# Attention inside a fused attention and expert kernel: the first score, transposition and value product of a group wait for the whole group

## The chip, the cores and the metric

The kernel runs on one core of one Trainium2 chip. Its time is what the device takes for one execution of the whole program, in microseconds (us); lower is better. TensorE (PE in the profile, PEld for its weight loads) multiplies matrices, VectorE (DVE), ScalarE (ACT) and GpSimd (POOL) work elementwise, SyncE (SP) issues transfers. Each engine works through its own queue in order, and engines wait for each other by semaphores.

## The reference

Three stages follow each other; what is changed lies in the first.

```python
scores = scale * np.matmul(q, k.transpose(0, 1, 3, 2))     # 4 sequences, 8 heads, 576 rows, 64 wide
scores = np.where(mask, scores + bias[None], -1000000000.0) # causal, window 128, slope per head
scores = scores - np.max(scores, axis=-1, keepdims=True)
attn = np.exp(scores)
attn = attn / (np.sum(attn, axis=-1, keepdims=True) + 1e-09)
out = np.matmul(attn, v)                                    # then reshaped to 2304 x 512
...
out += P[:, e:e + 1] * (np.maximum(x @ w1[e], 0.0) @ w2[e]) # 8 experts, gates P balanced by 8 rounds
...
return np.maximum(0.01 * h, h) @ w_out                      # h = x @ w_in
```

## The kernel before

The 2304 rows are 18 tiles of 128. Attention takes a tile in two groups of four heads (`steps`, 36 groups in all, `quad` 0 and 1). In a group, head `h = 4 * quad + 2 * n + r`: `n` is 0 or 1, and `r` says in which half of the 128 partitions the 64 values of the head lie (0: partitions 0 to 63, 1: 64 to 127), which is also the half of TensorE's rows that its score product uses.

For each group the kernel does the following.

- `scores` (L223 to L250): four products in float32 (L238), ordered n outer and r inner, write two PSUM tiles `s[0]` and `s[1]`, one for each `r`, each with both `n`. There are two such buffers, so the tiles of one group must be free before the next group writes them. Then for each head VectorE adds the distances and takes the row's minimum (L243, negated scores, so the minimum stands for the maximum), writing `e[r]`, and ScalarE takes the exponential of it in place with a sum (L247). Five buffers hold `e` tiles; a group takes two, and they come free when the group's transpositions have read them. A product shows as two TensorE records, since float32 goes through in two passes: a group has 8 records on L238.
- `probs_T` (L265): for each `r`, four transpositions on TensorE (L273) into `pt`, and one ScalarE copy to `pb` (L275).
- `values` (L278): eight products (L288), n outer, then key block, then r inner, into one PSUM tile `o` for the 8 heads of a tile; 16 records a group. A tile that starts a sequence has one key block, so its scores are 128 wide instead of 256 and its group has half the transpositions and value products.
- After the second group of a tile, `inverses` (L252) spreads the inverted row sums (L260), and VectorE scales the result into `acc` (L296).

The main loop (from L894 on) writes group s+1's scores ahead of group s's transpositions and values. Between them, `filling` sets in other jobs: the scaling and splitting of the first expert's weights (L553, L427, L428), then from the fifth tile on, steps of the first expert's two products (`a_steps`, L702, and `b_steps`, L819) for the tiles that are ready. All these jobs are emitted before attention ends; afterwards the kernel goes on with the other experts and the last network, where L702 and L819 make up nearly all of TensorE's work.

The order of the instructions in each engine's queue is not that of the program text alone. The kernel is built with `schedule_with_timeline_sim=True`: a planner goes through a simulated time line, and what stands earlier in the text goes first among what it holds ready. An instruction that it holds not yet ready is passed by others on its engine. The order is fixed when the kernel is built, and the chip keeps to it.

Of the kernel before, what the change touches and what calls it, by code (L numbers as in the profile page):

```python
# [13 lines left out]
AF = mybir.ActivationFunctionType  # L14
# [17 lines left out]
def attn_moe_kernel(  # L32
# [12 lines left out]
    nc = tc.nc  # L45
    P = 128
# [31 lines left out]
    ident = const.tile([P, P], F32, name="ident")  # L78
# [27 lines left out]
    for h in range(H):  # L106
        r = 64 * (h % 2)
# [6 lines left out]
    pools = {}  # L114

    anchors = {}

    def anchor():
        ins = nc.cur_bb.bb.instructions[-1]
        anchors[ins.engine] = ins  # L120
# [71 lines left out]
    st = {}  # L192
# [30 lines left out]
    def scores(i, quad):  # L223
        c = st[i]
        kb, qs = c["kb"], c["qs"]
        W = P * len(kb)
        c0 = 2 * P - W
        mn = ap2.tile([P, 4], F32, tag="mn", name="mn")
        if quad == 0:
            c["sm"] = ap2.tile([P, H], F32, tag="sm", name="sm")  # L230
        sm = c["sm"]
        s = [ps_s.tile([P, 2, 2 * P], F32, tag="s", name="s") for _ in range(2)]
        e = [ap1.tile([P, 2, 2 * P], F32, tag="e", bufs=5, name="e") for _ in range(2)]
        c[quad] = dict(e=e)
        for n in range(2):
            for r in range(2):
                h = 4 * quad + 2 * n + r
                nc.tensor.matmul(s[r][:, n, 0:W], qs[64 * r:64 * r + 64, h // 2, :],  # L238
                                 c["k"][64 * r:64 * r + 64, h // 2, 0:W], start=True, stop=True)
        for n in range(2):  # L240
            for r in range(2):
                h = 4 * quad + 2 * n + r
                nc.vector.tensor_tensor_reduce(  # L243
                    out=e[r][:, n, 0:W], in0=s[r][:, n, 0:W], in1=c["bias"][:, c0:], scale=2.0 ** (-8.0 * (h + 1) / H),
                    scalar=float(2**41), op0=ALU.add, op1=ALU.min, accum_out=mn[:, 2 * n + r:2 * n + r + 1],
                )
                nc.scalar.activation(  # L247
                    out=e[r][:, n, 0:W], in_=e[r][:, n, 0:W], func=AF.Exp, bias=mn[:, 2 * n + r:2 * n + r + 1],
                    scale=-1.0, accum_out=sm[:, h:h + 1],
                )  # L250

    def inverses(i):  # L252

        c = st[i]
        sm = c["sm"]
        nc.scalar.activation(out=sm, in_=sm, func=AF.Copy, bias=EPS)
        nc.vector.reciprocal(out=sm, in_=sm)
        rt = ps_t.tile([P, NP, P], F32, tag="pt", name="rt")
        for h in range(H):
            nc.tensor.matmul(rt[64 * (h % 2):64 * (h % 2) + 64, h // 2, :], sm[:, h:h + 1].to_broadcast([P, D]), ident,  # L260
                             start=True, stop=True)
        rb = c["rb"] = ap1.tile([P, NP, P], F32, tag="rb", name="rb")
        nc.scalar.activation(out=rb, in_=rt, func=AF.Copy)

    def probs_T(i, quad):  # L265
        c = st[i][quad]
        nb = len(st[i]["kb"])
        c["pb"] = []
        for r in range(2):
            pt = ps_t.tile([P, 2, 2, P], F32, tag="pt", name="pt")  # L270
            for n in range(2):
                for b in range(nb):
                    nc.tensor.transpose(pt[:, n, b, :], c["e"][r][:, n, b * P:(b + 1) * P], ident)  # L273
            pb = ap3.tile([P, 2, 2, P], F32, tag="pb", name="pb")
            nc.scalar.activation(out=pb[:, :, 0:nb, :], in_=pt[:, :, 0:nb, :], func=AF.Copy)  # L275
            c["pb"].append(pb)

    def values(i, quad):  # L278
        kb = st[i]["kb"]
        if quad == 0:  # L280
            st[i]["o"] = ps_o.tile([P, NP, P], F32, tag="o", name="o")
        o = st[i]["o"]
        pb = st[i][quad]["pb"]
        for n in range(2):
            for b, j in enumerate(kb):
                for r in range(2):
                    h = 4 * quad + 2 * n + r
                    nc.tensor.matmul(  # L288
                        o[64 * r:64 * r + 64, h // 2, :],
                        st[j]["v"][:, h * D:(h + 1) * D],  # L290
                        pb[r][:, n, b, :],
                        start=(b == 0), stop=(b == len(kb) - 1),
                    )
        if quad == 1:
            p = max(p for p, (t0, n) in enumerate(PAIRS) if t0 <= i)
            nc.vector.scalar_tensor_tensor(out=accT[i], in0=o, scalar=xin[p].sr[:, 0:1], in1=st[i]["rb"],  # L296
                                           op0=ALU.mult, op1=ALU.mult)
# [235 lines left out]
    W = [{}, {}]  # L533
# [342 lines left out]

    nc.sync.dma_start(wg, w_gate.rearrange("(k p) e -> p k e", p=P))
    scores(*steps[0])
    for job in input_scale(0):
        job()  # L880
# [13 lines left out]
    for s, (i, quad) in enumerate(steps):  # L894
# [11 lines left out]
        if s + 1 < len(steps):  # L906
            if quad == 1 and i + 2 < NTILE:
                load_qk(i + 2)
            if quad == 0 and 2 <= i + 1 < NTILE:
                load_v(i + 1)  # L910
            scores(*steps[s + 1])
# [6 lines left out]
        if scales:  # L918
            scales.pop(0)()
        probs_T(i, quad)  # L920
        if quad == 1:
            inverses(i)
        filling(left - 1)
        if scales:
            scales.pop(0)()
        values(i, quad)
    assert not fill
    for _ in range(8):
# [66 lines left out]
    for n, u in enumerate(units + [None]):  # L995
        a, b = [], b_steps(*prev)
# [9 lines left out]
        if prev[1] == ends[prev[0]] and prev[0] + 1 < NC:  # L1006
            k0 = len(b) - 7
            b = [[f] + ([lambda j=k - k0: W[1][prev[0] + 1].at(j)] if k >= k0 else []) for k, f in enumerate(b)]
        else:
            b = [[f] for f in b]  # L1010
# [70 lines left out]
```

## Time and profile before

| What | Value |
|---|---|
| time, median of 3 runs | 1960.12 us (1958.14 to 1960.9) |
| time of the profiled execution | 1959.59 us |
| its span, first to last instruction | 1957.8 us |
| VectorE busy | 1320.9 us (67%) |
| ScalarE busy | 1366.5 us (70%) |
| GpSimd busy | 1327.3 us (68%) |
| attention (L238, first to last start) | 5.0 to 221.8 us |

A busy share is the part of the span in which an engine had an instruction in hand. Matmuls are pipelined: the next one starts before the last one's modelled end, so what a stretch of them costs TensorE is read from one start to the next start, and the busy time of a piece reaches a little over it. A row of the time line merges neighbours of the same kind: `x8` are eight records, `[0.21 <-ACT pb L275]` is idle time before them and what ended it. In the view by windows each engine has its busy time and, in brackets, its instructions.

### The profile page before, as it was taken

How to read it: one execution, taken by the hardware profiler on the slowest of the kernel's cores; microseconds unless marked ns; L12 is line 12 of the kernel's file. 1: busy time of each engine (PE TensorE's matmuls, PEld its weight loads, DVE VectorE, ACT ScalarE, POOL GpSimd, SP SyncE). 2: the span in 40 equal slices, each digit the busy share in tenths (PEclk: the TensorE clock that was granted, in tenths of full speed). 3: DMA queues.
4: the chain of work that ended last, by engine and by line, in shares of the span. 5: the costliest groups of instructions: out<-in, count | busy, mean ns of one | idle time of the engine just before them, and what ended most of it. 6: DMA issues, size and time to landing. Idle time of an engine off the chain costs nothing.

```text
span 1957.8 us, 45103 instructions
## 1 busy us (share of the span) xinstructions
PE 1890.2 (97%) x17725; PEld 1626.5 (83%) x17725; DVE 1320.9 (67%) x3604; ACT 1366.5 (70%) x3123; POOL 1327.3 (68%) x1142
## 2 busy tenths in 40 slices
PE   8999988999999999999999999999999998999998
PEld 6777667888898888889888888889889877889897
DVE  6444466676776767677676767666666777677876
ACT  7977666776767666676767676676666778776764
POOL 3843275868787786878677686775767686666743
PEclk9999999999999999999999999999999999999999
DMA  8432001120211211120111112101000000001001
GB/s 269 125 87 71 12 12 55 39 62 32 82 47 47 66 39 55 39 82 28 66 65 40 55 39 66 44 2 45 23 23 23 23 23 23 24 22 44 2 28 71
DMA packets 57861, 97.80 MB, mean 50 GB/s; under 512 B 3632, under 2 KB 22064, under 8 KB 57648
## 3 DMA queue, kind: packets, MB, share of 16 engines
q1 hardware_dynamic: 57648, 94.92, 14.9%
q8 instruction: 138, 2.26, 0.5%
q14 instruction: 75, 0.61, 0.1%
HBM read 81.81 MB, written 13.11 MB: 48 GB/s over the span
## 4 chain that ended last, share of the span: by engine, by line
PE 78%; ACT 7%; DVE 5%; DMA 5%; POOL 3%; issue 2%; POOLq 0%; SPq 0%; ACTq 0%; DVEq 0%
PE t L819 35%; PE s L702 21%; PE sq L702 15%; DMA raw<-in_moe_w_dram 3%; PE s L238 2%; PE o L288 2%; PE pt L273 1%; ACT junk L550 1%; POOL h L775 1%; DVE s L731 1%; PE rt L260 1%; ACT raw L553 1%; ACT w L427 1%; ACT e L247 1%; ACT xp L427 1%
## 5 line engine op out<-in xcount | busy, mean ns | idle before, releaser
L819 PE MATMUL t<-w,h 128*128 128x256 f16 x7560 | 985.1, 273 | 22.9 <-ACT part L829 10.3
L702 PEld LDWEIGHTS <-w 128*128 128x128 f16 x8400 | 759.1, 98 | 120.3 <-issue 35.0
L819 PEld LDWEIGHTS <-h 128*128 128x128 f16 x7560 | 730.2, 98 | 125.6 <-issue 33.9
L702 PE MATMUL s<-xp,w 128*128 128x256 f16 (+1 forms) x4908 | 620.3, 263 | 20.3 <-ACT q L726 10.4
L832 DVE SCALAR_TENSOR_TENSOR acc<-t,pu,acc 128x256 f32<-128x256 f32 x864 | 407.9, 479 | 220.3 <-PE t L819 173.3
L775 POOL TENSOR_TENSOR h<-s,h 128x1024 f16<-128x1024 f32 x180 | 388.2, 2157 | 136.8 <-ACT h L772 95.7
L702 PE MATMUL sq<-xp,w 128*128 128x256 f16 (+1 forms) x3492 | 447.5, 262 | 6.2 <-ACT q L714 4.5
L830 POOL TENSOR_TENSOR acc<-acc,part 128x256 f32<-128x256 f32 x324 | 235.6, 729 | 292.9 <-ACT part L829 260.6
L428 POOL TENSOR_TENSOR w<-raw,w 128x512 f16<-128x512 f32 x240 | 277.7, 1168 | 42.3 <-ACT w L427 41.9
L731 DVE SCALAR_TENSOR_TENSOR h<-sq,h 128x512 f16<-128x512 f32 (+1 forms) x348 | 190.6, 552 | 82.4 <-ACT h L756 47.6
L829 ACT ACTIVATE part<-t,pu 128x256 f32<-128x256 f32 x324 | 152.5, 471 | 109.0 <-PE t L819 100.1
L772 ACT ACTIVATE h<-s 128x1024 f16<-128x1024 f32 x180 | 189.6, 1053 | 42.2 <-DVE s L731 41.3
L718 DVE SCALAR_TENSOR_TENSOR sq<-sq,q 128x256 f32<-128x256 f32 x348 | 148.4, 427 | 72.0 <-PE sq L702 57.0
L714 ACT ACTIVATE q<-s 128x256 f32<-128x256 f32 x366 | 138.3, 379 | 73.0 <-PE s L702 60.4
L427 ACT ACTIVATE w<-raw 128x512 f16<-128x512 f32 x240 | 148.2, 628 | 8.3 <-PE t L819 6.0
L731 DVE SCALAR_TENSOR_TENSOR s<-sq,s 128x256 f32<-128x256 f32 x348 | 145.1, 417 | 2.1
L750 ACT ACTIVATE h<-sq 128x512 f16<-128x512 f32 x174 | 103.2, 593 | 55.4 <-PE t L819 28.9
L731 DVE SCALAR_TENSOR_TENSOR s<-sq,q 128x256 f32<-128x256 f32 x348 | 130.3, 416 | 12.4 <-ACT q L726 10.6
L550 ACT ACTIVATE junk<-raw 128x512 bf16<-128x512 f32 x160 | 100.2, 626 | 48.2 <-DMA raw<-in_moe_w_dram 47.1
L718 DVE SCALAR_TENSOR_TENSOR sq<-s,q 128x256 f32<-128x256 f32 x174 | 74.5, 428 | 86.6 <-ACT q L714 78.2
L756 ACT ACTIVATE h<-sq 128x256 f16<-128x256 f32 x174 | 65.9, 379 | 65.1 <-DVE sq L718 58.2
L553 ACT ACTIVATE raw<-raw,sr 128x512 f32<-128x512 f32 x160 | 102.4, 714 | 3.8 <-DVE sr L422 3.4
(137 smaller groups left out, 1785.8 us busy)
## 6 DMA issues: line engine op xcount, KB each, us to landing
raw<-in_moe_w_dram SPq DMA_DIRECT2D x32, 1024.0 KB, 5.1
k_t<-in_k_dram SPq DMA_DIRECT2D x16, 512.0 KB, 3.8
raw<-in_moe_w_in_dram SPq DMA_DIRECT2D x16, 512.0 KB, 3.6
raw<-in_moe_w_out_dram SPq DMA_DIRECT2D x16, 512.0 KB, 3.5
q_t<-in_q_dram SPq DMA_DIRECT2D x18, 256.0 KB, 3.7
v_t<-in_v_dram SPq DMA_DIRECT2D x18, 256.0 KB, 2.7
acc<-in_v_dram SPq DMA_DIRECT2D x18, 256.0 KB, 6.6
out_dram<-acc SPq DMA_DIRECT2D x18, 256.0 KB, 2.0
```

The costliest lines, as they stand in the source:

```text
L427: nc.scalar.activation(out=hi, in_=src, func=AF.Copy)
L428: nc.gpsimd.tensor_tensor(out=lo, in0=src, in1=hi, op=ALU.subtract)
L702: nc.tensor.matmul(d[b][:, f, :], t[:, wp, kk, ft * P:(ft + 1) * P], XP[p][:, o, kk, xp, :], start=(i == 0 and f == 0 and j in FIRST), sto ...
L714: nc.scalar.activation(out=q[:, k], in_=ps, func=AF.Copy, scale=CS)
L718: nc.vector.scalar_tensor_tensor(out=block(k), in0=ps, scalar=CS, in1=q[:, k], op0=ALU.mult, op1=ALU.add)
L731: nc.vector.scalar_tensor_tensor(out=out, in0=in0, scalar=sc, in1=in1, op0=op0, op1=op)
L772: nc.scalar.activation(out=h[:, 3:7, 0, :], in_=d["s"], func=AF.Copy)
L775: nc.gpsimd.tensor_tensor(out=h[:, 3:7, 1, :], in0=d["s"], in1=h[:, 3:7, 0, :], op=ALU.subtract)
L819: nc.tensor.matmul(ps, h[:, o, hp, f, tt * P:(tt + 1) * P], w[:, wp, ft, :], start=(i == 0 and j in FIRST), stop=(i == 5), skip_group_chec ...
L829: nc.scalar.activation(out=part, in_=ps, func=AF.Copy, scale=s)
L830: nc.gpsimd.tensor_tensor(out=dst, in0=dst, in1=part, op=ALU.add)
L832: nc.vector.scalar_tensor_tensor(out=dst, in0=ps, scalar=s, in1=dst, op0=ALU.mult, op1=ALU.add)
```

## The change

`behind(ins, other)` makes an instruction wait for another. Four things are done with it or beside it.

- In `scores`, the first product (n = r = 0) waits for the last minimum of the group before.
- The minima and exponentials go r outer and n inner, instead of n outer and r inner: first both heads of `e[0]`, then both of `e[1]`.
- In `probs_T`, the first transposition of each `r` waits for the exponential of the second head of that `r`.
- In `values`, the first product waits for the copy of the second `pb` of its group.

No instruction is added to the arithmetic and none is taken away.

```diff
@@ -115,6 +115,11 @@
 
     anchors = {}
 
+    def behind(ins, other):
+
+        tc.add_manual_dep(ins.ins, other.ins.name, mybir.DependencyInfo(mybir.DependencyClass.Sync, mybir.DependencyReason.DATA),
+                          reason="whole group")
+
     def anchor():
         ins = nc.cur_bb.bb.instructions[-1]
         anchors[ins.engine] = ins
@@ -235,19 +240,23 @@
         for n in range(2):
             for r in range(2):
                 h = 4 * quad + 2 * n + r
-                nc.tensor.matmul(s[r][:, n, 0:W], qs[64 * r:64 * r + 64, h // 2, :],
-                                 c["k"][64 * r:64 * r + 64, h // 2, 0:W], start=True, stop=True)
-        for n in range(2):
-            for r in range(2):
+                ins = nc.tensor.matmul(s[r][:, n, 0:W], qs[64 * r:64 * r + 64, h // 2, :],
+                                       c["k"][64 * r:64 * r + 64, h // 2, 0:W], start=True, stop=True)
+                if n == r == 0 and "minimum" in st:
+                    behind(ins, st["minimum"])
+        exps = c[quad]["exps"] = []
+        for r in range(2):
+            for n in range(2):
                 h = 4 * quad + 2 * n + r
-                nc.vector.tensor_tensor_reduce(
+                st["minimum"] = nc.vector.tensor_tensor_reduce(
                     out=e[r][:, n, 0:W], in0=s[r][:, n, 0:W], in1=c["bias"][:, c0:], scale=2.0 ** (-8.0 * (h + 1) / H),
                     scalar=float(2**41), op0=ALU.add, op1=ALU.min, accum_out=mn[:, 2 * n + r:2 * n + r + 1],
                 )
-                nc.scalar.activation(
+                ins = nc.scalar.activation(
                     out=e[r][:, n, 0:W], in_=e[r][:, n, 0:W], func=AF.Exp, bias=mn[:, 2 * n + r:2 * n + r + 1],
                     scale=-1.0, accum_out=sm[:, h:h + 1],
                 )
+            exps.append(ins)
 
     def inverses(i):
 
@@ -270,9 +279,11 @@
             pt = ps_t.tile([P, 2, 2, P], F32, tag="pt", name="pt")
             for n in range(2):
                 for b in range(nb):
-                    nc.tensor.transpose(pt[:, n, b, :], c["e"][r][:, n, b * P:(b + 1) * P], ident)
+                    ins = nc.tensor.transpose(pt[:, n, b, :], c["e"][r][:, n, b * P:(b + 1) * P], ident)
+                    if n == b == 0:
+                        behind(ins, c["exps"][r])
             pb = ap3.tile([P, 2, 2, P], F32, tag="pb", name="pb")
-            nc.scalar.activation(out=pb[:, :, 0:nb, :], in_=pt[:, :, 0:nb, :], func=AF.Copy)
+            c["copied"] = nc.scalar.activation(out=pb[:, :, 0:nb, :], in_=pt[:, :, 0:nb, :], func=AF.Copy)
             c["pb"].append(pb)
 
     def values(i, quad):
@@ -285,12 +296,14 @@
             for b, j in enumerate(kb):
                 for r in range(2):
                     h = 4 * quad + 2 * n + r
-                    nc.tensor.matmul(
+                    ins = nc.tensor.matmul(
                         o[64 * r:64 * r + 64, h // 2, :],
                         st[j]["v"][:, h * D:(h + 1) * D],
                         pb[r][:, n, b, :],
                         start=(b == 0), stop=(b == len(kb) - 1),
                     )
+                    if n == b == r == 0:
+                        behind(ins, st[i][quad]["copied"])
         if quad == 1:
             p = max(p for p, (t0, n) in enumerate(PAIRS) if t0 <= i)
             nc.vector.scalar_tensor_tensor(out=accT[i], in0=o, scalar=xin[p].sr[:, 0:1], in1=st[i]["rb"],
```

## Rows read from the trace of the kernel before

**Rows 1.** The page's busy times over the span: share, instructions.

```profile
PE 1890.2 (97%) x17725; PEld 1626.5 (83%) x17725; DVE 1320.9 (67%) x3604; ACT 1366.5 (70%) x3123; POOL 1327.3 (68%) x1142
```

**Rows 2.** Windows: length, busy PE, PEld, DVE, ACT, POOL (instructions); clock, DMA, GB/s.

```profile
0.00:80.00 80.00, 72.05 (x528) 51.09 (x529) 42.17 (x202) 67.74 (x207) 45.48 (x61) 1.00 0.66 211
80.00:235.00 155.00, 153.40 (x1443) 112.97 (x1442) 79.29 (x279) 110.45 (x321) 55.06 (x49) 1.00 0.24 69
235.00:300.00 65.00, 52.22 (x529) 42.56 (x528) 36.62 (x109) 42.29 (x98) 45.48 (x40) 0.95 0.03 9
```

**Rows 3.** Windows of the score products alone (L238): PE, PEld.

```profile
0.00:80.00 80.00, 31.53 (x124) 19.61 (x124) 1.00 0.66 211
80.00:235.00 155.00, 34.83 (x164) 20.10 (x164) 1.00 0.24 69
```

**Rows 4.** Windows of the value products alone (L288): PE, PEld.

```profile
0.00:80.00 80.00, 17.62 (x176) 12.32 (x176) 1.00 0.66 211
80.00:235.00 155.00, 33.97 (x368) 23.45 (x368) 1.00 0.24 69
```

**Rows 5.** Time line of TensorE, 105 to 135 us: start, length, what, records.

```profile
108.91 0.43 PE L288 MATMUL o<-pb,v_t 128*64 128x128 f32 x2
109.28 0.66 PE L273 MATMUL pt<-ident,e 128*128 128x128 f32 x4
...
111.42 1.09 PE L288 MATMUL o<-pb,v_t 128*64 128x128 f32 x14
112.44 0.66 PE L273 MATMUL pt<-ident,e 128*128 128x128 f32 x4
...
113.25 1.14 PE L238 MATMUL s<-k_t,qs 64*128 64x256 f32 x8
114.32 0.88 PE L260 MATMUL rt<-ident,sm 128*64 128x128 f32 x12
...
115.81 1.13 PE L238 MATMUL s<-k_t,qs 64*128 64x256 f32 x4
...
123.17 1.13 PE L238 MATMUL s<-k_t,qs 64*128 64x256 f32 x4
124.23 0.83 PE L819 MATMUL t<-w,h 128*128 128x256 f16 x6
```

**Rows 6.** Time line of all engines, 155 to 170 us: TensorE's rows.

```profile
160.50 1.09 PE L288 MATMUL o<-pb,v_t 128*64 128x128 f32 x16
...
161.53 0.87 PE L273 MATMUL pt<-ident,e 128*128 128x128 f32 x6
...
163.53 1.13 PE L238 MATMUL s<-k_t,qs 64*128 64x256 f32 x6
...
164.59 0.50 PE L819 MATMUL t<-w,h 128*128 128x256 f16 x3
...
165.03 0.70 PE L238 MATMUL s<-k_t,qs 64*128 64x256 f32 x2
...
165.65 0.87 PE L260 MATMUL rt<-ident,sm 128*64 128x128 f32 x10
```

**Rows 7.** Windows of the minima alone (L243, with their reads): DVE.

```profile
80.00:235.00 155.00, 31.62 (x172) 1.00 0.24 69
```

**Rows 8.** Windows of the exponentials alone (L247, with reads): ACT.

```profile
80.00:235.00 155.00, 46.17 (x172) 1.00 0.24 69
```

**Rows 9.** TensorE's separate waits for L238: least/median/most ns.

```profile
L238 PEldq EVENT_SEMAPHORE  x16: 51/51/2665, 4.6 to 206.7; - x16
```

**Rows 10.** Waits from 0 to 80 us: total us, times, longest.

```profile
DVE e L243 <- PE pt L273: 9.5, 4, 5.6
```

**Rows 11.** Chain of waits, 225 to 300 us: start, us, what.

```profile
232.55 0.67 DVE acc L296
233.37 2.59 ACT xp L427 x6
...
241.98 2.88 DVE sx L474 x3
```

## The prediction, made before the changed kernel was built or run

> **What bounds the kernel now.** I read the page's busy times first: TensorE has an instruction in hand 97% of the span and no other engine over 70% [rows 1]. The change touches only attention, so I cut its stage out by windows [rows 2]. The reader is to see three parts. Up to 80 us TensorE has only 528 records and ScalarE is busy 67.7 of 80 us. From 80 to 235 us TensorE is busy 153.4 of 155 us with 1443 records, ScalarE 110.5, VectorE 79.3, GpSimd 55.1: here TensorE's queue is the bound, because attention's products share it with the first expert's (L702, L819). From 235 to 300 us TensorE falls to 52.2 of 65.
>
> Then I looked at what TensorE's time is spent on, in the time line, from one start to the next. A whole score group, eight records that alternate between the two halves of the rows, takes 114.32 - 113.25 = 1.07 us. Half a group, four records that all use one half of the rows, takes 124.23 - 123.17 = 1.06 us [rows 5]. So a half costs as much as a whole: products on different row halves run beside each other, products on the same half one after the other. The halves of that group started at 115.81 and 123.17, 7.36 us apart, with other work between. The planner had held `s[0]` ready first, sent its two products alone, and `s[1]`'s later.
>
> The value products have the same fault in small. A whole group of 16 takes 161.53 - 160.50 = 1.03 us [rows 6]. Sent as 2 (waiting for the second `pb`) and later 14, it takes 109.28 - 108.91 = 0.37 and 112.44 - 111.42 = 1.02, so 1.39 us [rows 5], 0.36 more.
>
> **The change part by part.** *First score waits for the last minimum of the group before.* That minimum frees `s[1]`, so at that moment both PSUM tiles are free and all four products are ready at once; in the program's order they alternate the row halves. Price now: L238 is busy 34.83 us from 80 to 235 us in 164 records [rows 3], which is 20.5 groups. Whole they would be busy 20.5 x 1.14 = 23.4 us (1.14 is the busy time of the x8 row of [rows 5]). The difference is 11.5 us, in about 11 pieces too many, and each piece's busy time reaches 0.07 us over the next start (1.13 against 1.06), so 11.5 - 0.8 = 10.7 us of TensorE's queue. A second kind of cut may stay. Five of the twenty groups there are cut into six and two records with an expert's work between them, as at 163.53 and 165.03: both halves were ready and the planner still set something in. That costs 164.59 - 163.53 + 165.65 - 165.03 = 1.68 us against 1.07 [rows 6], 0.61 each, 3.0 in all, which I leave in. Left: 7.7 us.
>
> *First value product waits for the second copy.* L288 is busy 33.97 us in 368 records from 80 to 235 us [rows 4], 23 groups; whole they would be busy 23 x 1.09 = 25.1 us [rows 6]. Of the 8.9 us difference, about 21 pieces too many count 0.07 us each twice (1.09 against 1.02 in [rows 5]), 1.5 us. Left: 7.4 us. The copy of the second `pb` ends the wait of the other 14 now, so they start no later; the first two are late by 0.37 us at most.
>
> *First transposition waits for the second exponential.* Four transpositions stay the unit, as most of them stand now (x4 in [rows 5]), so I count nothing. Bounds: 2 us gained where pairs now go alone, 2 us lost where a pair could have filled a hole.
>
> *Minima by row halves.* Four minima and four exponentials a group, before and after: nothing added. A head's minimum takes 31.62 / 86 = 0.37 us and its exponential 46.17 / 86 = 0.54 us [rows 7, 8]. The exponentials that the first transpositions need come second instead of third, 0.54 us sooner; those of the other half come at the same time. Nothing on the path of a full TensorE: 0, with 0.37 us a group as the bound either way.
>
> *The waits themselves.* 35 on scores, 72 on transpositions and 36 on value products. Each first instruction waits for the same engine already, so I expect a higher count in a wait that is there. If each became a separate wait of TensorE's sequencer it would cost 143 x 0.051 = 7.3 us [rows 9]; I take 0, since only 16 such stand before L238's 288 records now, and keep 7.3 as the end. Behind a waiting score stand, in TensorE's own queue, whatever the planner put there: transpositions, values, L702, L819; for these wait ScalarE's copies and VectorE's evacuations. From 80 us on the planner has expert products to put ahead of the score; that is the cover. Without it a group loses the lead of its first half: two minima and two exponentials, 2 x 0.37 + 2 x 0.54 = 1.8 us.
>
> *Before 80 us.* L238 is busy 31.53 us in 124 records where 15.5 whole groups would be 17.7, so up to 13.8 us lie there too [rows 3], and about 3 more in the values. But ScalarE is busy 67.7 of 80 us [rows 2], and attention waits for its exponentials and copies. The Trainium skill, TensorEngine Tiling (Array Packing), section Performance Considerations, says that tiling speeds up TensorE but not the emptying of PSUM, which may become the bound. By that rule these 80 us give nothing, by TensorE's rows up to 17; ScalarE's row here is on the rule's side. I take 0 and keep 10 for the range, since ScalarE's first 80 us hold weight splitting that could be done after.
>
> *After attention.* The chain from 232.55 us goes from the last scaling into `acc` to the splits of the last tiles (ACT xp, DVE sx) [rows 11]. It begins when attention ends and moves with it, so what attention gains is not given back there.
>
> **The sum.** 7.7 + 7.4 = 15.1 us off the profiled execution's 1959.59 (span 1957.8 plus 1.8 around it): 1944.5 us. The median of the runs shown is 0.5 us over the profiled one, so I forecast **1945 us**. What is late next: with 15 us less, ScalarE is busy 110.5 of 140 us, 79%, still under TensorE.
>
> **The rivals.**
> *The order stays cut.* The planner still sets expert steps and older attention work between the products, because these stand earlier in the text. For it: the five groups in six and two. Against it: only half-ready tiles make the four-and-four cut, and this goes. If half of the gain stays away: 1959.6 - 7.5 = 1952 us.
> *ScalarE or the seam takes the gain.* ScalarE's queue, already full before 80 us, holds `pb` and `e` back, or the weights of the next expert end the stretch from 235 to 300 us whatever attention does. For it: TensorE is only 80% busy there [rows 2]. Against it: the chain there starts at attention's last tile [rows 11], and ScalarE has 45 us free between 80 and 235. Then 1960 us, within 2 of before.
> *The lost lead counts before 80 us.* Here hardly any expert product can cover a waiting score. A group's last minima can themselves wait for TensorE, since `e` buffers come free only with transpositions: 9.5 us in four waits, the longest 5.6 [rows 10]. Now a whole score group stands behind such a minimum, where half of it went ahead before. If each of the 16 groups there loses the 1.8 us worked out above, that is 29 us against 15 gained: 1974 us at the worst, 1967 if three quarters are lost. It decides from 15.1 / 16 = 0.94 us a group on. Against it: the second half waited for that minimum before too, and a group's values need both halves.
> *It does nothing.* If the planner already held the scores for whole tiles, nothing would move; the four-and-four cuts speak against that, and I give this no chance of its own beside the second rival.
>
> **How the numbers follow.** Forecast (most pieces become whole) 0.58, order stays cut 0.18, gain taken away 0.12, lost lead 0.12. About 0.2%, 3.9 us, is what a measurement of this kernel can tell from no change. The first two are faster by more than that, with a little left over in the second: faster 0.75. The third is the same, with that little: same 0.14. The fourth, less its mildest cases: slower 0.11. The range goes down to what the stretch before 80 us could add and the cuts in six and two could still give, 1944.5 - 10 - 3 = 1931.5, so 1931; up, over the second rival and the third, to 1963, which holds the mildest third of the lost lead. About 0.08 lies above it and 0.07 below.
>
> **What would show it.** The score group as x8 in TensorE's time line with 1.07 us to the next start, and L238 busy some 24 to 27 us instead of 34.83 for 164 records; L288 as x16, busy near 25 for 368. Attention's last score starts some 15 us before 221.8, most of it won after 80 us, and the stretch after attention keeps its length. Expert products per 20 us rise while scores and values shrink. Wrong would be: TensorE idle before L238 on DVE mn by more than some 5 us in all, which is the lost lead; ScalarE near full after 80 us; x4 rows as many as before; or an earlier end of attention with the same end of the kernel.

## The result and the profile after

The changed kernel took **1944.09 us** (median of 4 runs, 1942.43 to 1946.49), the kernel before on the same chip 1960.51 us (4 runs, 1958.14 to 1963.2): a ratio of 0.9917, with a 95% interval of 0.99 to 0.9934. The profiled execution took 1944.12 us with a span of 1942.3, 15.5 us less than the one before. The forecast of 1945 us was met; the way to it was not. Line numbers after the change: scores L243, minima L251, exponentials L255, transpositions L282, copy L286, values L299, first expert L715 and L832.

The page's busy times, beside [rows 1]: TensorE's fell by 30.7 us and VectorE's by 3.8, with as many records.

```profile
PE 1859.5 (96%) x17725; PEld 1610.0 (83%) x17725; DVE 1317.1 (68%) x3604; ACT 1365.9 (70%) x3123; POOL 1329.4 (68%) x1142
```

The windows of [rows 2], after the change (same columns):

```profile
0.00:80.00 80.00, 55.82 (x472) 39.89 (x474) 40.99 (x196) 62.45 (x192) 44.94 (x61) 0.94 0.64 211
80.00:235.00 155.00, 148.98 (x1557) 113.70 (x1554) 80.73 (x290) 118.86 (x346) 63.91 (x56) 1.00 0.23 69
235.00:300.00 65.00, 53.39 (x539) 44.28 (x537) 38.60 (x117) 43.95 (x105) 43.32 (x39) 0.97 0.03 9
```

Two things happened. From 80 to 235 us TensorE does 1557 records instead of 1443 in less busy time: that was forecast. Up to 80 us it does 472 instead of 528 and is busy 55.8 us instead of 72.1: there the kernel fell behind. So attention's last value row starts only 7.1 us sooner, 223.80 against 230.88 us, and not 15. A second trace of the same changed kernel (after_again, below) has that row at 225.02 us, so ends of attention that lie 1 us apart are not told apart here.

```profile
214.00 1.13 PE L243 MATMUL s<-k_t,qs 64*128 64x256 f32 x8
...
223.80 1.09 PE L299 MATMUL o<-pb,v_t 128*64 128x128 f32 x16
```

```profile
221.09 1.13 PE L238 MATMUL s<-k_t,qs 64*128 64x256 f32 x4
...
230.88 1.09 PE L288 MATMUL o<-pb,v_t 128*64 128x128 f32 x14
```

The other 8.4 us came long after attention. I counted TensorE's records back from the end of the program, where the instructions of both kernels stand in the same order, and took the difference of the start times: -7.1 us at 290 to 350 us, -6.2 at 650, -10.1 at 710, -12.9 at 945, -14.4 at 1052, and -15.55 from 1200 us on. So 0.9 us of attention's gain was lost again by 650 us, and then work that the diff doesn't touch became faster in four steps: 3.9 us in the first, 5.4 in the other three.

### The profile page after: what moved, and what is told of

Its sections match the earlier page's. It is cut to its first block, busy times and chain, and to the rows that moved or that the text cites. A ratio compares the mean times of both kernels' runs of the same rounds, so it can differ in the third digit from the quotient of the medians.

```text
span 1942.3 us, 45092 instructions
## 1 busy us (share of the span) xinstructions
PE 1859.5 (96%) x17725; PEld 1610.0 (83%) x17725; DVE 1317.1 (68%) x3604; ACT 1365.9 (70%) x3123; POOL 1329.4 (68%) x1142
## 4 chain that ended last, share of the span: by engine, by line
PE 77%; ACT 7%; DMA 5%; DVE 4%; POOL 3%; issue 2%; SPq 0%; POOLq 0%; DVEq 0%; ACTq 0%
PE t L832 35%; PE s L715 21%; PE sq L715 15%; DMA raw<-in_moe_w_dram 3%; PE o L299 1%; ACT junk L563 1%; PE s L243 1%; PE pt L282 1%; DVE s L744 1%; ACT e L255 1%; ACT raw L566 1%; POOL h L788 1%; ACT w L440 1%; DMA acc<-in_v_dram 1%; POOL xp L441 1%
## 5 line engine op out<-in xcount | busy, mean ns | idle before, releaser
L832 PE MATMUL t<-w,h 128*128 128x256 f16 x7560 | 980.7, 273 | 21.0 <-ACT part L842 9.5
L715 PEld LDWEIGHTS <-w 128*128 128x128 f16 x8400 | 759.2, 98 | 120.2 <-issue 33.8
L832 PEld LDWEIGHTS <-h 128*128 128x128 f16 x7560 | 729.0, 98 | 120.8 <-issue 32.1
L715 PE MATMUL s<-xp,w 128*128 128x256 f16 (+1 forms) x4908 | 618.2, 262 | 24.0 <-ACT q L739 10.5
L715 PE MATMUL sq<-xp,w 128*128 128x256 f16 (+1 forms) x3492 | 447.5, 262 | 4.1 <-DVE s L744 1.6
L744 DVE SCALAR_TENSOR_TENSOR s<-sq,q 128x256 f32<-128x256 f32 x348 | 130.2, 415 | 12.4 <-ACT q L739 10.6
```

The costliest lines, as they stand in the source:

```text
L715: nc.tensor.matmul(d[b][:, f, :], t[:, wp, kk, ft * P:(ft + 1) * P], XP[p][:, o, kk, xp, :], start=(i == 0 and f == 0 and j in FIRST), sto ...
L744: nc.vector.scalar_tensor_tensor(out=out, in0=in0, scalar=sc, in1=in1, op0=op0, op1=op)
L832: nc.tensor.matmul(ps, h[:, o, hp, f, tt * P:(tt + 1) * P], w[:, wp, ft, :], start=(i == 0 and j in FIRST), stop=(i == 5), skip_group_chec ...
```

## Where the second half came from

At each step a transfer had been slow in the kernel before. The trace has packets that are marked as instructions, in queues apart from the data's: 138 of 16 KB in one queue and 75 smaller ones in another. In the kernel before a packet of 16 KB begins inside each of the four slow transfers; after the change the packets at the three writes begin near the end of the write or outside it. Worked out from the packed trace (us; a write of `wout` that nothing delays takes 2.0, the median of 16):

```
                         before                        after
transfer           issued   took  packet at     issued   took  packet at
load of raw        695.81   7.30     696.00     689.33   5.17     689.87
write of wout      927.44   3.63     928.38     917.27   2.19     919.13
write of wout     1041.24   4.02    1042.18    1028.44   2.05    none inside
write of wout     1190.13   3.17    1190.91    1175.52   2.00    1177.29
```

A packet of the other queue lies in two of these slow writes as well, 2.7 us after the issue of 927.44 and 2.2 us after that of 1190.13, but none lies in the slow write of 1041.24, so those are not needed for it.

The write is what the next load waits for (its buffer `raw` is free only then), and on that load hangs the chain. The two chains through one such place, before and after: start, us, what.

```profile
930.35 0.61 ACT raw L643
930.96 0.20 ACT q L714
931.16 4.97 DMA raw<-in_moe_w_dram
...
939.19 0.93 PE s L702 x6
```

```profile
918.85 0.69 ACT h L785
919.54 5.15 DMA raw<-in_moe_w_dram
...
928.64 0.81 PE s L715 x6
```

From the write's issue to the load's it is 931.16 - 927.44 = 3.72 us before and 919.54 - 917.27 = 2.27 after. In the waits of the transfers' queue (us in total, times, longest) that is the row of the load on the write, here before and after:

```profile
SPq L546 <- DMA wout<-raw: 22.7, 11, 3.6
```

```profile
SPq L559 <- DMA wout<-raw: 18.2, 11, 1.8
```

A packet that begins in a write may slow it, or both may only have come together by chance. TensorE's queue has 35493 records in the kernel before, 257 for each of the 138 packets, so which packet falls where should follow the count of instructions ahead of it in that queue. The change altered that count without adding arithmetic: the trace has 32 separate waits of TensorE's sequencer where it had 40, so TensorE's queue is 8 instructions shorter. That could be tried.

## The experiments

Each gives its median, and its ratio to the kernel before on the same chip with the 95% interval. "Attention" is the start of the last value row. Three theories were open on the first gain: that the alternation of the row halves is what makes a whole group cheap (A), that standing next to each other is enough (E), and that the score wait alone does nearly all (B). On the second gain: that the instruction packets make it (F), or that it is chance of each build (G).

**score_only: the score wait alone**, minima in the old order.

```diff
-        for r in range(2):
-            for n in range(2):
+        for n in range(2):
+            for r in range(2):
...
-                    if n == b == 0:
-                        behind(ins, c["exps"][r])
...
-                    if n == b == r == 0:
-                        behind(ins, st[i][quad]["copied"])
```

> The score wait alone: the first score product of a group waits for the last minimum of the group before; minima keep their old order, transpositions and values their old waits. Theory A (whole score groups save TensorE's time from 80 us on, and the wait costs the lead of the first half before 80 us): from 80 to 235 us score groups stand as x8 and L-score is busy about 27 us for 170 records instead of 34.8 for 164, some 9 us saved there; before 80 us TensorE stands idle before scores for the last minimum, as it does in the changed kernel (6.2 us in three waits), and some 6 us are lost. Time 1952 to 1960 us. Rival B (the score wait is the whole gain, the rest is decoration): 1944 to 1947 us.

Measured: 1944.45 us (5 runs), ratio 0.9937 [0.9925, 0.9949]; attention 225.55 us. Scores and values from 80 to 235 us:

```profile
80.00:235.00 155.00, 25.86 (x168) 14.71 (x168) 0.99 0.22 69
```

```profile
80.00:235.00 155.00, 34.31 (x384) 24.25 (x384) 0.99 0.22 69
```

The scores are as cheap as with the whole change, the values as dear as before, and the time, inside rival B's range, can't be told from the whole change's. The values' share of the forecast isn't seen in the end.

**value_only: the value wait alone**, minima in the old order.

```diff
-                if n == r == 0 and "minimum" in st:
-                    behind(ins, st["minimum"])
...
-                    if n == b == 0:
-                        behind(ins, c["exps"][r])
```

> The value wait alone: the first value product of a group waits for the second copy. Theory A: from 80 to 235 us the value products are busy some 29 us for 384 records instead of 34.0 for 368, TensorE's queue is 7 us shorter, and nothing is lost before 80 us: 1951 to 1955 us. Rival C (merging two records with fourteen saves nothing, since the two fill time that is a wait anyway): 1958 to 1962 us.

Measured: 1956.29 us (12 runs, 1949.41 to 1962.8), ratio 0.9991 [0.9979, 1.0004]; attention 244.91 us, 14 us later than before. The value records did become cheaper (30.22 us for 384 from 80 to 235 us, 29 expected), but the time lies in neither theory's range. What no theory had: the new order starves TensorE early, and its clock falls towards the lower of its two levels (1.2 of 2.4 GHz). Windows, columns as in [rows 2]:

```profile
20.00:40.00 20.00, 17.09 (x100) 12.16 (x98) 15.80 (x59) 13.86 (x45) 4.28 (x4) 0.63 0.83 272
40.00:60.00 20.00, 20.00 (x88) 13.37 (x87) 5.68 (x32) 11.80 (x35) 2.52 (x3) 0.51 0.23 68
```

At 0.51 an engine that is "busy" 20 of 20 us does 88 records. Some 9 of the 14 us were won back later, since in this build the four transfers are not slowed: what the kernel before does from 290 to 1260 us, in 970 us, takes 960.8 us here and 961.9 after the change. The trace is that of the longest of the 12 runs, 1962.8 us, 3.2 us over the profiled run of the kernel before. So a time near before's hides two large effects of opposite sign.

**minima_only: the minima by row halves alone.**

```diff
-                if n == r == 0 and "minimum" in st:
-                    behind(ins, st["minimum"])
...
-                    if n == b == 0:
-                        behind(ins, c["exps"][r])
...
-                    if n == b == r == 0:
-                        behind(ins, st[i][quad]["copied"])
```

> The order of minima and exponentials alone (r outer, n inner), no added wait. Theory A: no gain on a full TensorE, 1958 to 1962 us; the score groups stay cut in four and four. Rival D (the sooner exponentials of the first row half, or the earlier release of the first PSUM tile, carry part of the gain): under 1956 us.

Measured: 1956.84 us (11 runs), ratio 1.0 [0.9992, 1.0009]. Nothing, as forecast. TensorE's queue is as long as before's here, and the slow writes are where before's are (924.97, 1038.64 and 1187.54 us: 3.37, 3.95 and 4.16 us).

**same_half: the whole change, but the score products r outer**, so that products of one half stand together.

```diff
-        for n in range(2):
-            for r in range(2):
+        for r in range(2):
+            for n in range(2):
                 h = 4 * quad + 2 * n + r
                 ins = nc.tensor.matmul(s[r][:, n, 0:W], qs[64 * r:64 * r + 64, h // 2, :],
```

> The changed kernel whole, but with the four score products of a group in the order r outer, n inner, so that neighbours use the same row half: the group still goes as one piece of eight records and has the same waits. Theory A (the saving is that products on different row halves run beside each other): a group takes 2.1 us to the next start instead of 1.07, twenty groups from 80 us on cost about 21 us more: 1962 to 1970 us, no better than the kernel before. Rival E (the saving is in fewer pieces and fewer switches between kinds of products): 1943 to 1948 us.

Measured: 1940.2 us (4 runs, 1939.45 to 1942.58), ratio 0.9915 [0.9903, 0.9928]. Its whole groups cost what alternating ones cost, 118.29 - 117.22 = 1.07 us:

```profile
117.22 1.14 PE L243 MATMUL s<-k_t,qs 64*128 64x256 f32 x8
118.29 0.65 PE L299 MATMUL o<-pb,v_t 128*64 128x128 f32 x6
```

In that group the first two records start at 117.221 and 117.235 us and the rest follow in such pairs. Two products of one half can't do that: the four records of 1.06 us in [rows 5] start over 200 ns apart. So the second half's start beside the first's. The records don't name the row half, but the queue of this kernel, as it was built, has both products of the first half ahead of both of the second in this group, and the trace bears that out where a group is cut: a piece of four costs 1.06 us here, as two products of one half do, and 0.63 in the changed kernel, where a piece of four holds both halves. The first two rows are of same_half, the others of the changed kernel:

```profile
143.88 1.13 PE L243 MATMUL s<-k_t,qs 64*128 64x256 f32 x4
144.94 0.83 PE L715 MATMUL s<-xp,w 128*128 128x256 f16 x6
```

```profile
137.50 0.70 PE L243 MATMUL s<-k_t,qs 64*128 64x256 f32 x4
138.13 0.83 PE L832 MATMUL t<-w,h 128*128 128x256 f16 x6
```

Theory A falls: it is not the alternation that counts but that both halves stand together in the queue.

**after_again: the changed kernel as it is**, as the base of the next runs.

> The changed kernel once more, timed on the same chip as the three kernels beside it. Its profile showed that attention ended only some 7 us sooner (last value products at 223.8 instead of 230.9 us) and that 8 us more were won between 690 and 1200 us, where both kernels issue the same instructions. Theory F (four transfers there take 1 to 2 us longer in the kernel before, because a fetch of TensorE's instructions falls into each of them, and in the changed kernel not): the same trace again, no slow transfer among these four, 8 to 9 parts in a thousand faster. Rival G (the four slow transfers were chance): they come and go from run to run, and the median lies 7 us under the kernel before.

Measured: 1944.23 us (5 runs), ratio 0.9923 [0.9911, 0.9936]; attention 225.02 us. The load (688.76 us) takes 5.23 us and the three writes 2.35, 2.03 and 1.99, as F expected.

**after_pad4 and before_pad20: shift the queue only.** At the start of the program a few products of one column are added, 2 instructions each, into a tile that nothing reads: 4 to the changed kernel (8 instructions, what the change had taken away), 20 to the kernel before (40 instructions).

```diff
     nc.vector.tensor_copy(identb, ident)
+    pad = ps_a.tile([1, P], F32, tag="s1", name="pad")
+    [nc.tensor.matmul(pad, identb[:, 0:1], identb, start=True, stop=True) for _ in range(4)]
```

> The changed kernel with four small products (8 instructions, into a tile that nothing reads) at the start of TensorE's queue, where it waits for inputs anyway. The changed kernel has 8 TensorE records fewer than the one before (35485 against 35493), so this puts the blocks of its instruction stream back where they lie in the kernel before; all other engines have the same order. Theory F (fetches that fall into transfers): the transfers at about 689, 917, 1031 and 1177 us take 1 to 2 us longer again, and the time rises by 5 to 8 us over the changed kernel. Rival G (chance, or something else in the change): the time of the changed kernel, within 2 us.

> The kernel before with twenty such products (40 instructions) at the start of TensorE's queue: its fetches come some 2.3 us sooner (256 records of TensorE take about 14.5 us from 300 us on), so before the four slow transfers begin. Attention as before. Theory F: the four transfers fall to 5.2 and 2.0 us, the time falls by 5 to 8 us under the kernel before, unless the fetches now meet other transfers. Rival G: the time of the kernel before, within 2 us.

Measured: 1949.88 us (5 runs), ratio 0.995 [0.9937, 0.9962], and 1952.38 us (5 runs), ratio 0.9966 [0.9952, 0.9979]. Eight more instructions make the changed kernel 5.65 us slower, forty make the old one 5.9 us faster, and neither moves attention's end much (its last value record starts at 223.8 and 232.9 us, without padding at 224.6 and 231.7). TensorE's row for 690 to 1210 us, of before, after, after_pad4 and before_pad20 in this order:

```profile
690.00:1210.00 520.00, 508.55 (x4817) 449.00 (x4815) 363.14 (x924) 358.45 (x774) 392.78 (x330) 0.99 0.16 54
```

```profile
690.00:1210.00 520.00, 513.98 (x4901) 455.60 (x4898) 367.90 (x938) 364.48 (x788) 400.12 (x337) 1.00 0.16 53
```

```profile
690.00:1210.00 520.00, 508.70 (x4838) 450.16 (x4836) 364.04 (x926) 360.57 (x782) 392.95 (x330) 1.00 0.16 52
```

```profile
690.00:1210.00 520.00, 513.95 (x4900) 455.57 (x4899) 368.84 (x942) 367.11 (x792) 397.88 (x334) 1.00 0.16 54
```

TensorE's busy time has two values, 508.6 and 514.0, some 5.4 us apart, and the padding swaps them. The load's wait on the write swaps too, first after_pad4, then before_pad20:

```profile
SPq L559 <- DMA wout<-raw: 24.7, 11, 4.0
```

```profile
SPq L546 <- DMA wout<-raw: 17.8, 11, 1.7
```

In after_pad4 the packets begin 0.8 to 1.0 us into the writes of 913.92, 1027.92 and 1177.02 us, which take 4.43, 3.90 and 4.04; in before_pad20 they begin 1.1 to 1.3 us ahead of the writes of 926.69, 1037.67 and 1185.05, which take 2.0 each. For the three writes theory F is shown, both ways, and G falls. For the load it is not: after_pad4 was to have a slow one again, but its load of 685.97 us takes 5.07 us, with a packet 0.35 us in. What after_pad4 loses it loses at the three writes, which are slower there than in the kernel before (12.4 us together against 10.8).

**late_waits: the three waits only from the ninth tile on** (`i >= 8`), to keep the early order and the late gain.

```diff
-                if n == r == 0 and "minimum" in st:
+                if n == r == 0 and "minimum" in st and i >= 8:
...
-                    if n == b == 0:
+                    if n == b == 0 and i >= 8:
...
-                    if n == b == r == 0:
+                    if n == b == r == 0 and i >= 8:
```

> The changed kernel with all three waits only from the ninth tile on (group 16, some 84 us), the new order of minima everywhere. Theory H (the waits gain 14 us on a full TensorE after 80 us and lose 7 us before 80 us, where TensorE has nothing else to do): attention's last value products end some 14 us before those of the kernel before, at about 217 us, against 223.8 in the changed kernel. Rival I (the stage before 80 us loses nothing, the gain after it is 7 us): they end at about 224 us. The whole time follows, less or plus what the four transfers do: 1930 to 1945 us by H, 1940 to 1950 by I.

Measured: 1949.75 us (5 runs), ratio 0.9955 [0.9942, 0.9967]; attention 222.79 us, 8.1 us sooner than before and not clearly sooner than the whole change (223.80 and 225.02), where theory H expected 217 and rival I 224. The early stretch is that of before, but a score record and a value record from 80 us on are dearer than after the whole change (values 29.90 us for 368; scores below), with some groups still cut in 2, 4 and 2:

```profile
80.00:235.00 155.00, 29.16 (x164) 15.67 (x164) 1.00 0.24 69
```

```profile
127.05 0.70 PE L243 MATMUL s<-k_t,qs 64*128 64x256 f32 x2
...
129.09 0.70 PE L243 MATMUL s<-k_t,qs 64*128 64x256 f32 x4
...
130.31 0.70 PE L243 MATMUL s<-k_t,qs 64*128 64x256 f32 x2
```

It also has slow writes (915.73, 1030.01 and 1179.08 us: 3.88, 3.87 and 4.08 us).

**early_waits: the three waits only up to the eighth tile** (the same edit with `i < 8`).

```diff
-                if n == r == 0 and "minimum" in st:
+                if n == r == 0 and "minimum" in st and i < 8:
...
-                    if n == b == 0:
+                    if n == b == 0 and i < 8:
...
-                    if n == b == r == 0:
+                    if n == b == r == 0 and i < 8:
```

> The changed kernel with all three waits only up to the eighth tile (groups 0 to 15), the new order of minima everywhere: what the waits do before some 84 us, alone. Theory J (before 80 us the waits cost about 5 us, because TensorE has no other work while a group waits; after 80 us they gain 8 to 12): attention's last value products end 3 to 7 us after the 230.9 us of the kernel before, at about 236 us, and TensorE is busy some 15 us less from 0 to 80 us. Rival K (the idle time there costs nothing, since ScalarE and the transfers set the pace): they end at 229 to 232 us. The whole time follows by the same amount, plus or minus up to 7 us by where the fetches fall.

Measured: 1958.65 us (12 runs, 1955.36 to 1960.72), ratio 0.999 [0.9982, 0.9998]; attention 237.69 us, 6.8 us later than before. So without the late waits the early ones cost 6.8 us (theory J), and adding the late ones to them, which makes the whole change, brings 237.69 - 223.80 = 13.9 us. The other way round the late waits alone bring 8.1 us (late_waits), and adding the early ones to them costs 223.80 - 222.79 = 1.0 us. So the two don't add, and 6.8 is the most that the early waits cost. The time is still that of before, since here the three writes aren't slowed (2.23, 2.04 and 2.00 us) and the step at the load is there as well.

**late_pad20: late_waits with the 20 products** that helped the kernel before.

```diff
     nc.vector.tensor_copy(identb, ident)
+    pad = ps_a.tile([1, P], F32, tag="s1", name="pad")
+    [nc.tensor.matmul(pad, identb[:, 0:1], identb, start=True, stop=True) for _ in range(20)]
```

> The waits from the ninth tile on only, as measured at 1949.75 us, with the twenty small products at the start of TensorE's queue that took the slow transfers out of the kernel before. Theory F: the expert stage between attention's end and 1260 us falls from 989 to some 981 us, the time to about 1942.5 us. Rival L (the twenty products helped the kernel before in another way, for instance by warming TensorE's clock at the start): no shorter expert stage, 1948 to 1951 us.

Measured: 1944.2 us (5 runs), ratio 0.9922 [0.9909, 0.9934]: 5.55 us under late_waits, which ran on another chip, and its three writes take 2.0 us each. F again, in a third kernel, and rival L falls.

**late_same_pad20: late_pad20 with the score products r outer**, all that had helped in one kernel.

```diff
-        for n in range(2):
-            for r in range(2):
+        for r in range(2):
+            for n in range(2):
                 h = 4 * quad + 2 * n + r
                 ins = nc.tensor.matmul(s[r][:, n, 0:W], qs[64 * r:64 * r + 64, h // 2, :],
```

> As the last one, with the four score products in the order r outer, n inner, which measured 1940.2 us in the changed kernel. If the gain of that order (attention 1 to 2 us shorter, expert stage 3 us shorter) adds to the others: 1936 to 1941 us. If it was luck in the planner's order: 1942 to 1946 us.

Measured: 1962.08 us (12 runs, 1956.37 to 1968.25), ratio 1.0014 [1.0, 1.0027]; attention's last value record is at 248.1 us. The planner made another early order, with a granted clock of 0.51 from 40 to 60 us, as in value_only. The gains don't add, and no version here is shown to be faster than the changed kernel: same_half has the lowest median, with an interval that overlaps it.

## Why the prediction was right, and where it was not

*Whole groups after 80 us: right.* The group of eight with 1.07 us to the next start became the usual one, 14 of the 19 groups of 256 columns that start after 80 us:

```profile
113.34 1.14 PE L243 MATMUL s<-k_t,qs 64*128 64x256 f32 x8
114.41 1.09 PE L269 MATMUL rt<-ident,sm 128*64 128x128 f32 x16
...
119.85 1.13 PE L243 MATMUL s<-k_t,qs 64*128 64x256 f32 x8
120.92 1.48 PE L832 MATMUL t<-w,h 128*128 128x256 f16 x12
```

L243 is busy 26.86 us for 176 records, inside the 24 to 27 forecast [rows 3]; L299 28.73 for 384 against "near 25 for 368" [rows 4]:

```profile
80.00:235.00 155.00, 26.86 (x176) 14.94 (x172) 1.00 0.23 69
```

```profile
80.00:235.00 155.00, 28.73 (x384) 21.46 (x384) 1.00 0.23 69
```

From start to next start, idle time left out, a score record costs 144.6 ns instead of 198.1, a value record 69.3 instead of 83.4: (198.1 - 144.6) x 172 = 9.2 us and (83.4 - 69.3) x 384 = 5.4 us, 14.6 together. The score term had been put at 7.7, the value term at 7.4, so the one was too small and the other too large. That the halves alternate, as the prediction has it, isn't needed (same_half). And what the cheaper values are worth in the time isn't shown: score_only, without them, ends attention at 225.55 us, 0.5 us behind the second trace of the whole change.

*"Before 80 us: I take 0": the step that failed.* The rival of the lost lead came true in part, not by its 1.8 us a group but by at most 6.8 us in all, which early_waits shows by itself; beside the late waits it is 1.0. By 80 us TensorE is 56 records behind (472 against 528). The sign that was named for it, TensorE idle before scores on VectorE's minimum for over 5 us, is there; waits up to 80 us, total, times, longest:

```profile
PEld s L243 <- DVE mn L251: 7.8, 6, 4.7
PE s L243 <- DVE mn L251: 6.2, 3, 4.5
```

One score group makes up most of it:

```profile
30.78 2.08 PE L243 MATMUL s<-k_t,qs 64*128 64x256 f32 x8 [4.50 <-DVE mn L251]
```

It waits 4.50 us for the last minimum of the group before, where half of it went ahead before the change. That minimum stood in VectorE's queue behind reductions of `acc` (L226), of which three had waited 1.50, 0.79 and 0.48 us for their loads. Then the group takes 2.08 us where such a group takes 1.14: after six nearly idle microseconds TensorE runs at the lower of its two levels. Columns as in [rows 2]:

```profile
24.00:30.00 6.00, 1.31 (x8) 0.84 (x8) 5.25 (x15) 3.06 (x10) 1.90 (x2) 0.89 1.05 382
30.00:33.00 3.00, 2.22 (x10) 1.40 (x12) 3.00 (x13) 2.17 (x8) 0.00 (x0) 0.50 1.08 320
33.00:36.00 3.00, 3.00 (x22) 2.27 (x20) 2.56 (x12) 1.44 (x6) 1.04 (x1) 0.57 0.71 207
36.00:40.00 4.00, 4.00 (x47) 3.16 (x46) 2.48 (x16) 3.21 (x13) 0.00 (x0) 1.00 0.25 72
```

The clock stood at 1.00 through these 80 us before [rows 2], and I had no term for it. ScalarE, which I had named as the bound there, is busy less than before (62.45 against 67.74 us), and it lost most of that from 20 to 40 us, where the long wait stands. From 40 to 60 us it is nearly full in both kernels, so that it can't make up for it, and TensorE waits for its copies. The two windows before and after, and two rows of TensorE after the change:

```profile
20.00:40.00 20.00, 19.33 (x174) 14.20 (x174) 18.29 (x77) 18.52 (x60) 5.44 (x5) 1.00 0.90 296
40.00:60.00 20.00, 19.88 (x142) 13.93 (x141) 10.67 (x59) 19.27 (x56) 14.35 (x15) 1.00 0.42 120
```

```profile
20.00:40.00 20.00, 12.84 (x104) 9.05 (x101) 15.27 (x65) 13.89 (x48) 4.24 (x4) 0.83 0.85 280
40.00:60.00 20.00, 15.28 (x148) 10.98 (x146) 9.78 (x55) 19.91 (x54) 14.94 (x15) 1.00 0.36 106
```

```profile
60.75 1.09 PE L269 MATMUL rt<-ident,sm 128*64 128x128 f32 x16 [2.65 <-ACT pb L286]
...
62.73 1.88 PE L299 MATMUL o<-pb,v_t 128*64 128x128 f32 x16 [0.89 <-ACT pb L286]
```

So the bound was read rightly and the 0 drawn from it was wrong: a wait that leaves the bound without work costs its time. This is read from the rows; no run separates the wait, the clock and the planner's new order. Whole groups did save TensorE time there: L243 is busy 19.54 us for 116 records instead of 31.53 for 124 [rows 3], and the stretch gained nothing by it. The Trainium skill, TensorEngine Tiling (Array Packing), section Performance Considerations, says that tiling doesn't speed up the emptying of PSUM; the missing gain and the waits of 2.65 and 0.89 us for ScalarE's copies agree, but what the score waited 4.50 us for was one minimum, and the rule has no loss.

*"After attention: not given back there": too little.* Only 0.9 us was given back by 650 us, and 9.3 us came on top, for which I had no term. The 5.4 us at the three writes come from instruction packets that no longer delay them: after_pad4, before_pad20 and late_pad20 move the end by 5.65, 5.9 and 5.55 us. The 3.9 us around the load are not explained by this.

*The waits themselves at 0, with 7.3 us as the end:* no cost seen. Scores still have 16 separate waits ahead of 288 records [rows 9], and TensorE as a whole has 8 fewer.

*Transposition and minima at 0:* right for the minima (minima_only). The transposition's wait wasn't tried alone; score_only, which lacks it and the value wait, runs in the same time as the whole.

So the number is better than the reasoning, by luck. Attention brought 7.1 us of the 15.1 (5.9 by the second trace), and the 8.4 us that make up the rest came where the forecast had 0. The sum for the stretch after 80 us, 15.1, measured 13.9 on top of early_waits and 8.1 without them.

*Open:* why the planner's order from 80 us on is worse in late_waits, whose waits there are the same ones. And the first of the four steps, at the load of 695.81 us: its packet falls inside in both kernels, 0.2 us and 0.5 us after the issue, and only one is slow (7.30 against 5.17 us), so that a packet begins inside a transfer isn't by itself enough. The second trace of the changed kernel has one at 0.26 us and takes 5.23. The slow load is 2.1 us of the step's 3.9.

## What to carry to other kernels

When a planner sets the order, a wait added in one place makes a new order everywhere: judge it by stages, since a gain where TensorE's queue is full and a loss where it is starved came from the same three waits here, and the two didn't add. A dependency that keeps the products of both row halves together in the queue is worth about 1 us for each group that would be sent in two halves (1.07 us instead of 2.1 for eight records), in whichever order the program writes them. And before a difference of some 5 us is put down to an edit, look where in the program it arises: if in work that the edit doesn't touch, shift the instruction queue by a few harmless instructions and see whether it moves.

## What was not expected of the hardware

- Packets of instructions delay the data's transfers. One that began about 1 us into a write of 256 KB stretched it from 2.0 to between 3.2 and 4.4 us, and in a chain of write, load and product the end of the kernel moved by 5.6 to 5.9 us for 8 or 40 instructions more in TensorE's queue. One that began near a write's end (1.8 us in) left it at 2.0 to 2.4 us.
- A wait of 4.5 us, in six microseconds with 1.31 us of TensorE's work, cost more than itself: the granted clock was 0.50 from 30 to 33 us and 0.57 from 33 to 36, and the next products took nearly twice their time (2.08 us for 1.14).
- Score products on the other half of the rows started 14 ns after those of the first half, with both products of the first half ahead of them in the queue (same_half); that these pairs are of different halves is worked out from the starts, since the records don't name the half.
